# Diagonal sums moved from TensorE to GpSimd and VectorE, k tiles of the first six units loaded four tokens to a partition, and a new order of work

## The chip, the cores and the metric

The kernel runs on one core of one Trainium2 chip. The metric is the time of one execution on the device in microseconds (us), the median of several runs. A core has five engines that run their own instruction queues: TensorE (PE, with its weight loads listed apart as PEld), VectorE (DVE), ScalarE (ACT), GpSimd (POOL) and SyncE (SP). They share the on-chip memory SBUF; matmul results land in PSUM, eight banks of 128 x 512 f32. DMA transfers between HBM and SBUF are issued from the queues of SP, POOL and ACT.

## The reference

Two stages. The first is a linear-attention recurrence with a decay per channel (4 batches, 8 heads, 768 tokens, head size 48); the second is a feed-forward block with a squared ReLU (384 to 2048 to 384).

```python
for t in range(S):
    cur = np.einsum('bhd,bhe->bhde', u[None] * kt, vt)
    y[:, :, t] = np.einsum('bhd,bhde->bhe', rt, state + cur)
    state = w[None, :, :, None] * state + np.einsum('bhd,bhe->bhde', kt, vt)
...
h = x @ w_in
g = np.maximum(h, 0.0) ** 2
out = g @ w_out
```

`x` is `y` with the heads side by side: 3072 tokens by 384.

## The kernel before

**Tiling.** The tokens are cut into chunks of 128. There are 6 chunks times 4 batches = 24 units, numbered `i`, chunk by chunk, the four batches of a chunk next to each other. A unit holds 128 tokens on the partitions and 8 heads x 48 = 384 columns.

**A unit's attention steps.** `load` brings r, k and (units 0 to 5) v by SP; from unit 6 on `load_v` brings v by POOL, after a one-column copy named `gate` that waits until the k tile of the unit before has landed. `scale` (DVE, L470/L473) multiplies r and k by powers of w and writes them in bf16 into `rkw`. `rkw` is turned so that channels lie on the partitions: units 0 to 5 by TensorE (`turn`, L499) with two ACT copies out of PSUM (`evict_rk`), later ones by a DMA transpose (`turn_dma`, L488). The result is `rkT`. `at` (L521, 8 matmuls) forms the products of all token pairs, and `mask` (DVE, L533, twice) keeps those with the key earlier than the query.

The diagonal term, a token's own key and value, is made apart from that. `rk` (DVE, L513) multiplies the r half of `rkT` by the k half, and four matmuls in `sums` (L541) contract that with `uwb`, which holds u times w. This gives one sum per token and head in the same PSUM bank as the chunk's state sums (L546). `diag_v` (DVE, L555) multiplies v by it. `state_add`, `state_decay` (DVE, L559, L563) and `state_cast` (ACT, L567) carry the state on. `y_mm` (L576, L582) forms y, `evict_y` (DVE, L591) adds the diagonal term and gives `yb`, and `yb` is turned into `xT` by TensorE (units 0 to 5, L607 and L611) or by DMA (L600).

**The feed-forward steps.** `mm1` (L623) runs in 96 groups, each a PSUM bank of 512 columns; then `relu` on ACT (L631) and `square` on ACT (L638) or, for one in four, on DVE (L640). `mm2` (L647; L663 for the last unit) has four groups of four matmuls for each unit, then an ACT copy (L654) and a store from SP.

**Weights.** Eight weight transfers (`weights`, L454 to L460) are issued from POOL. Each comes after a one-column `gate` copy that waits for one of the first loads, listed in `FRONT`.

**What sets the order.** A planner at build time (`Plan`) lists every step with its engine, a cost and what it needs. It plays the list through and writes each engine's instructions in the order so found. An engine executes its queue strictly in that order. A step's due time is its `rank`, replaced for some steps by a number in the table `TURNS`. Until a set planned time, TensorE's queue is filled with matmuls on a constant tile (`fill`, L404) wherever nothing is ready; each such matmul stays in the queue as an instruction. `room` limits how many buffers of each kind are alive.

Of the kernel before, what the change touches and what calls it, by code (L numbers as in the profile page):

```python
# [166 lines left out]
def kernel(  # L167
# [11 lines left out]
    nc = tc.nc  # L179
# [9 lines left out]
    NPE = 6  # L189
    NPY = 6  # L190
# [5 lines left out]
        "I": {  # L196
            0: 144.24, 1: 1, 2: 2, 3: 4
        },
        "rt": {
            0: -131.984, 1: -82.502, 10: 20.43, 11: 21.618, 12: 25.547, 13: 27.498, 17: 47.129, 18: 50.413, 2:  # L200
            -71.138, 20: 58.225, 21: 61.113, 22: 65.692, 23: 68.66, 3: -70.253, 4: -15.411, 5: -7.144, 6: -9.444, 7:
            -6.312
        },
        "kt": {
            0: -136.858, 1: -115.745, 11: 20.876, 16: 39.093, 17: 48.35, 19: 50.948, 2: -73.584, 21: 62.596, 3:
            -25.052, 4: -13.87, 5: -1.455, 7: 11.897
        },
        "vt": {
            0: -88.087, 1: -127.327, 2: -116.777, 3: -14.463, 4: -11.435
        },  # L210
        "sadd": {
            0: -35.242, 12: 43.151, 17: 67.289, 18: 102.058, 6: 13.355, 9: 51.499
        },
        "at": {
            10: 28.41, 15: 48.663, 2: -1012.58, 21: 75.098, 22: 80.521, 23: 97.568, 3: -57.886, 5: -85.117, 9: 73.42
        },
        "dv": {
            11: 56.999, 12: 34.611, 18: 78.368, 2: -30.837, 3: -9.083, 7: -23.381, 9: 47.89
        },
        "scale": {  # L220
            (11, 0): 45.098, (18, 0): 85.344, (23, 0): 137.198, (3, 1): 16.099, (7, 1): 36.154
        },
        "sums": {
            11: 42.348, 15: 32.285, 18: 118.116, 20: 60.674, 21: 90.506, 22: 104.529, 3: -90.968, 4: -96.114, 7:
            36.606
        },
        "stb": {
            11: 51.142, 12: 48.384, 15: 79.952, 18: 64.365, 19: 104.678, 3: -21.476, 8: 67.092
        },
        "xturn": {  # L230
            3: -95.414
        },
        "xT": {
            3: -7.841, 7: 22.027
        },
        "turn": {
            (4, 1): -1019.11, (5, 1): -65.755
        },
        "rkT": {
            (4, 0): 27.124  # L240
        },
        "sdec": {
            11: 61.243, 14: 47.641, 5: 39.993, 7: 39.494, 9: 46.764
        },
        "mask": {
            (16, 0): 82.669, (8, 0): 37.716
        },
        "y": {
            11: 43.284, 12: 43.282, 13: 71.578, 19: 65.5, 22: 88.724, 9: 26.437
        },  # L250
        "rk": {
            11: 57
        },
        "yb": {
            12: 49.359, 17: 87.282
        },
        "vb": {
            14: 76.055, 16: 78.861, 22: 86.101
        },
        "relu": {  # L260
            (0, 1): 29.661, (1, 2): 26.789, (10, 7): 52.135, (12, 5): 79.181, (16, 7): 91.168, (18, 3): 87.004, (2,
            1): 27.188, (2, 2): -7.03, (20, 0): 75.975, (20, 2): 81.329, (6, 0): 46.77, (7, 1): 40.936, (8, 1):
            30.757, (8, 6): 69.828
        },
# [10 lines left out]
        },  # L275
# [8 lines left out]
        },  # L284
        "out": {
            0: 23, 1: 27.877, 10: 69.852, 11: 74.396, 12: 68.581, 13: 44.909, 15: 66.178, 2: 31.669, 7: 43.746, 9:
            60.995
        },
        "sq": {
            (1, 2): 73.636, (10, 6): 70.251, (14, 3): 47.259, (16, 3): 88.397, (16, 5): 101.673, (18, 4): 49.326,  # L290
            (20, 0): 71.116, (20, 1): 86.752, (20, 2): 83.213, (6, 2): 58.323, (7, 1): 11.056, (8, 2): 53.53
        },
        "osb": {
            11: 86.148, 16: 91.532, 8: 76.964
        },
        "O": {
            0: 3, 1: 5, 2: 6, 3: 7
# [3 lines left out]
        ("I", 1, ("kt", 3)), ("I", 2, ("rt", 1)), ("O", 0, ("rt", 4)), ("I", 3, ("vt", 0)),  # L301
        ("O", 1, ("rt", 4)), ("O", 2, ("kt", 4)), ("O", 3, ("vt", 4)), ("I", 0, ("vt", 2)),
# [69 lines left out]
    wfour = const.tile([128, 4, 2, D], F32)  # L372
# [3 lines left out]
    spread = {}  # L376

# [21 lines left out]
    gate = const.tile([128, 1], F32)  # L399

# [52 lines left out]
    def weights(gated, q, which):  # L453
        nc.gpsimd.tensor_copy(gate, tiles[gated[1]][gated[0]][:, 0, :1])  # L454
# [7 lines left out]
    def pair(x):  # L462
        return x.rearrange("p (a o) d -> p a o d", o=2)

    def scale(i, x):
        t = tiles[i]
        t["rkw"] = rkw_b[i % NPAD]
        if x or i >= NPE:
            src, wx = (t["kt"], wneg) if x else (t["rt"], wpos)
            nc.vector.tensor_tensor(t["rkw"][:, x, :, :, :D], pair(src), pair(wx), ALU.mult)  # L470
        else:
            got = t["rt"].rearrange("p (o l) d -> p l o d", o=2)
            nc.vector.tensor_tensor(t["rkw"][:, 0, :, :, :D], got, wfour, ALU.mult)  # L473

    def load_v(i):
        c, b = units[i]
        nc.gpsimd.tensor_copy(gate, tiles[i - 1]["kt"][:, 0, :1])  # L477
# [23 lines left out]
    def evict_rk(i, x):  # L501
        t = tiles[i]
        if x:
            nc.scalar.copy(t["rkT"][:, 1], t["tp", 1])  # L504
        else:
            nc.scalar.copy(
                t["rkT"][:, 0].rearrange("p a (q l) -> p a q l", l=4), t["tp", 0].rearrange("p l (q a) -> p a q l", a=HP)
            )

# [25 lines left out]
    def sums(i):  # L535
# [3 lines left out]
        t["d"] = bank("s", i)[:, dm : dm + H]  # L539
        for p in range(HP):  # L540
# [4 lines left out]
        for p in range(HP if c < NCH - 1 else 0):  # L545
# [3 lines left out]
                start=False, stop=(p == HP - 1), skip_group_check=True,  # L549
# [148 lines left out]
    add("w", ACT, 1.08, power_four, rank=-1e3, needs=["w0"])  # L698
    add("wk", ACT, 0.48, do(power, wneg, down), rank=-999, needs=["log", "w"], uses=[("log", n) for n in range(4)])
# [7 lines left out]
    for n, (what, q, gated) in enumerate(FRONT):  # L707
# [3 lines left out]
        )  # L711
    for i in range(NU):
# [4 lines left out]
        for n, name in enumerate(("rt", "kt", "vt") if i < NPE else ("rt", "kt")):  # L717
            swift = n == 0 and i < NPE
# [5 lines left out]
        for x in range(2):  # L724
            add(
                ("scale", i, x), DVE, 0.47, do(scale, i, x), rank=a - 4 + 0.1 * x,
                needs=[("rt", i) if x == 0 else ("kt", i), "wk" if x else ("w" if i < NPE else "wr"), ("scale", i - 1, x) if i else None],
# [149 lines left out]
```

## Time and profile before

| | |
|---|---|
| median of 3 runs | 178.01 us (176.65 to 178.38) |
| the profiled execution's own time | 177.58 us |
| its span, first to last instruction | 175.8 us |
| granted TensorE clock | 1.00 throughout |
| DMA traffic | 28.88 MB, 86838 packets, of which 77632 are under 512 bytes |

The page of the profile sums each engine's busy time and lists groups of equal instructions with their count, busy time and mean duration. A view by windows gives each engine's busy time in chosen stretches; a timeline lists instructions in order of time. A matmul's listed duration holds a latency that the next matmul overlaps: four matmuls of one kind in a row are listed with 0.39 us and eight with 0.62 us, so that each further one takes about 0.06 us. The same holds for DVE, whose listed 0.55 us for a 384-column instruction is 0.47 us from one start to the next. Costs are therefore taken from one start to the next.

### The profile page before, as it was taken

Reading aid. Unit: us, or ns where it says so; the run is one execution under the profiler, and the core shown is the slowest. Engines: PE = TensorE matmul, PEld = TensorE weight load, DVE = VectorE, ACT = ScalarE, POOL = GpSimd, SP = SyncE. Lnnn points to the kernel's source line nnn. Section 1 sums busy time; section 2 is a strip of 40 time slices with the busy share of each in tenths; the row PEclk is TensorE's granted clock in tenths of the full one; section 3 lists DMA queues with packets and bytes.
Section 4 is the critical chain, followed back from the end, with each engine's and each line's share of the span. In section 5 each row is a group of like instructions: output and inputs, shape, how many; then the busy total and the mean of one; then the engine's idle time right before and its main releaser. Section 6 shows DMA issues by size and latency. Waiting matters only on the chain.

```text
span 175.8 us, 5172 instructions
## 1 busy us (share of the span) xinstructions
PE 168.0 (96%) x2096; PEld 131.8 (75%) x2096; DVE 120.9 (69%) x244; ACT 129.8 (74%) x264; POOL 34.8 (20%) x80
## 2 busy tenths in 40 slices
PE   6997999899999999999999999999999999999992
PEld 5986888777777777787876776866866977777972
DVE  3277977745699999987979878889896356540300
ACT  3628799997749396799797595795894897584950
POOL 7570090005402220203213023202211000000000
PEclk9999999999999999999999999999999999999999
DMA  4989999999999999899899999995999924031022
GB/s 111 204 160 191 230 152 212 184 205 188 134 183 165 193 173 206 181 164 215 188 206 177 270 202 194 150 240 130 209 185 151 313 54 132 4 110 24 4 92 87
DMA packets 86838, 28.88 MB, mean 164 GB/s; under 512 B 77632, under 2 KB 85952, under 8 KB 86816
## 3 DMA queue, kind: packets, MB, share of 16 engines
q1 hardware_dynamic: 81744, 21.83, 67.5%
q0 software_dynamic: 4928, 6.69, 21.4%
q8 instruction: 16, 0.26, 0.6%
q14 instruction: 6, 0.05, 0.1%
q10 hardware_dynamic: 144, 0.05, 0.1%
HBM read 20.50 MB, written 4.72 MB: 143 GB/s over the span
## 4 chain that ended last, share of the span: by engine, by line
PE 62%; DMA 24%; SPq 5%; DVE 3%; POOL 2%; issue 2%; ACT 1%; DVEq 0%; POOLq 0%
PE bank L623 28%; PE bank L647 25%; DMA w_out_q<-in_moe_w_out_dram 8%; DMA kt<-in_k_dram 6%; DMA xT<-yb 5%; DMA rkT<-rkw 4%; SPq L448 3%; PE bank L521 2%; SPq L450 2%; PE bank L576 2%; PE bank L663 2%; PE bank L582 1%; POOL w_out_q L460 1%; PE bank L546 1%; PE bank L541 1%
## 5 line engine op out<-in xcount | busy, mean ns | idle before, releaser
L623 PE MATMUL bank<-xT,w_in_q 128*128 128x128 bf16 (+1 forms) x864 | 71.7, 237 | 1.0 <-ACT xT L611 0.5
L631 ACT ACTIVATE gr<-bank 128x512 f32<-128x512 f32 x96 | 54.6, 609 | 21.9 <-PE bank L623 21.9
L647 PE MATMUL bank<-w_out_q,g 128*128 128x384 bf16 x368 | 68.0, 326 | 0.3 <-DMA w_out_q<-in_moe_w_out_dram 0.3
L623 PEld LDWEIGHTS <-w_in_q 128*128 128x128 bf16 x864 | 61.0, 98 | 7.0 <-issue 0.8
L647 PEld LDWEIGHTS <-g 128*128 128x128 bf16 x368 | 33.5, 98 | 19.1 <-issue 0.4
L638 ACT ACTIVATE g<-gr 128x512 bf16<-128x512 f32 x72 | 45.1, 650 | 0.7
L533 DVE TENSOR_TENSOR am<-bank,smask 128x512 bf16<-128x512 f32 x48 | 31.4, 683 | 8.6 <-PE bank L521 8.1
L640 DVE TENSOR_TENSOR g<-gr 128x512 bf16<-128x512 f32 x24 | 16.5, 686 | 14.6 <-ACT gr L631 14.5
L477 POOL COPY gate<-kt 128x1 f32<-128x1 f32 x18 | 5.2, 290 | 81.1 <-DMA kt<-in_k_dram 81.1
L470 DVE TENSOR_TENSOR rkw<-kt,wneg 128x384 bf16<-128x384 f32 x24 | 13.2, 551 | 6.6 <-ACT wneg L416 3.4
L479 POOL DMA_DIRECT2D vt<-in_v_dram x18 | 15.9, 884 | 4.2 <-issue 1.3
L567 ACT CAST stb<-st 128x384 bf16<-128x384 f32 x20 | 10.6, 528 | 7.9 <-DVE st L559 4.4
L654 ACT COPY osb<-bank 128x384 f32<-128x384 f32 x23 | 11.1, 483 | 5.4 <-PE bank L647 5.3
L555 DVE TENSOR_TENSOR dv<-vb,bank 128x384 f32<-128x384 bf16 x24 | 13.0, 547 | 2.8 <-PE bank L546 1.6
L513 DVE TENSOR_TENSOR rk<-rkT 128x512 bf16<-128x512 bf16 x24 | 10.1, 419 | 6.9 <-ACT rkT L504 4.9
L591 DVE TENSOR_TENSOR yb<-bank,dv 128x384 bf16<-128x384 f32 x24 | 13.2, 550 | 1.9 <-PE bank L582 1.4
L483 ACT CAST vb<-vt 128x384 bf16<-128x384 f32 x24 | 12.5, 520 | 0.0
L404 PE MATMUL bank<-warm 128*128 128x128 bf16 x116 | 11.0, 268 | 1.1 <-DVE warm L342 1.1
L470 DVE TENSOR_TENSOR rkw<-rt,wpos 128x384 bf16<-128x384 f32 x18 | 9.9, 550 | 1.0 <-DMA rt<-in_r_dram 1.0
L404 PEld LDWEIGHTS <-warm 128*128 128x128 bf16 x116 | 9.6, 124 | 1.3 <-DVE warm L342 1.1
L521 PE MATMUL bank<-rkT 64*128 64x128 bf16 x192 | 9.6, 220 | 0.2 <-DMA rkT<-rkw 0.2
L521 PEld LDWEIGHTS <-rkT 64*128 64x128 bf16 x192 | 5.5, 95 | 5.6 <-issue 3.7
(71 smaller groups left out, 123.1 us busy)
## 6 DMA issues: line engine op xcount, KB each, us to landing
kt<-in_k_dram SPq DMA_DIRECT2D x24, 192.0 KB, 4.2
out_dram<-osb SPq DMA_DIRECT2D x23, 192.0 KB, 2.6
rt<-in_r_dram SPq DMA_DIRECT2D x18, 192.0 KB, 4.3
vt<-in_v_dram POOLq DMA_DIRECT2D x18, 192.0 KB, 4.8
w_in_q<-in_moe_w_in_dram POOLq DMA_DIRECT2D x4, 384.0 KB, 7.4
w_out_q<-in_moe_w_out_dram POOLq DMA_DIRECT2D x4, 384.0 KB, 11.3
rt<-in_r_dram SPq DMA_DIRECT2D x12, 96.0 KB, 3.9
vt<-in_v_dram SPq DMA_DIRECT2D x6, 192.0 KB, 4.9
```

The costliest lines, as they stand in the source:

```text
L404: nc.tensor.matmul(out=banks[0][:, :128], lhsT=warm, rhs=warm, start=True, stop=True)
L470: nc.vector.tensor_tensor(t["rkw"][:, x, :, :, :D], pair(src), pair(wx), ALU.mult)
L479: nc.gpsimd.dma_start(out=tiles[i]["vt"], in_=v[b, :, c * C : (c + 1) * C, :].rearrange("h s d -> s h d"))
L521: nc.tensor.matmul(out=t["at"][o][:, p, :], lhsT=t["rkT"][sl, 1, p, :], rhs=t["rkT"][sl, 0, p, :], start=True, stop=True,)
L533: nc.vector.tensor_tensor(am, t["at"][o], smask.unsqueeze(1).to_broadcast([C, HP, C]), ALU.mult)
L555: nc.vector.tensor_tensor(t["dv"], t["vb"], t["d"].unsqueeze(2).to_broadcast([C, H, D]), ALU.mult)
L591: nc.vector.tensor_tensor(t["yb"], t["y"], t["dv"].rearrange("p h d -> p (h d)"), ALU.add)
L623: nc.tensor.matmul(out=t["h", s][:, a], lhsT=turned, rhs=chunks[c]["xT"][:, n, b : b + m, :], start=(n == 0), stop=(n == NK - 1),)
L631: nc.scalar.activation(t["gr", s], t["h", s], AF.Relu)
L638: nc.scalar.activation(g, x, AF.Square)
L640: nc.vector.tensor_tensor(g, x, x, ALU.mult)
L647: nc.tensor.matmul(out=t["o"], lhsT=chunks[units[i][0]]["g"][:, f, units[i][1], :], rhs=w_out_q[f // 4][:, f % 4, :], start=(f == 0), stop ...
```

## The change

Three things are done, and all queues are put in a new order.

1. The k tiles of units 0 to 5 are loaded as the r tiles already were: four consecutive tokens on a partition, in two transfers with 768 contiguous bytes a descriptor instead of one with 192. `scale` then multiplies k by a second set of powers with that layout (`wfour[:, 1]`), `evict_rk` restores the order of the tokens while it copies, and because the state sums need k with tokens in order, `rkT`'s k half is turned back by four matmuls (`turn_back`) and copied by ACT into `rkw` (`evict_back`). The powers are made by two DVE multiplications or additions and two ACT exponentials of 384 columns in place of four of 96.
2. From unit 6 on `rk` and the four matmuls with `uwb` are gone. GpSimd multiplies r by k and the product by u (`product`, two instructions of 128 x 384 f32), and DVE sums 48 columns at a time (`product_sum`). `diag_v` now reads that sum from SBUF, not PSUM. u is loaded once to all partitions (`load_u`, one gate and one transfer on POOL). In the last chunk, units 20 to 23, `sums` is left out altogether.
3. `TURNS` and `FRONT` are new. The gate copies read the last head's column, not the first's.

```diff
+    NKE = 6
+    ND = 6
     TURNS = {
...
     FRONT = (
-        ("I", 1, ("kt", 3)), ("I", 2, ("rt", 1)), ("O", 0, ("rt", 4)), ("I", 3, ("vt", 0)),
-        ("O", 1, ("rt", 4)), ("O", 2, ("kt", 4)), ("O", 3, ("vt", 4)), ("I", 0, ("vt", 2)),
+        ("I", 0, ("kt", 0)), ("I", 1, ("rt", 1)), ("O", 0, ("rt", 2)), ("I", 2, ("kt", 4)),
+        ("O", 1, ("vt", 4)), ("I", 3, ("kt", 3)), ("O", 2, ("vt", 3)), ("O", 3, ("rt", 5)),
     )
...
-    def power_four():
-        for l in range(4):
-            nc.scalar.activation(wfour[:, l].rearrange("p o d -> p (o d)"), lnw, AF.Exp, scale=at4[:, l : l + 1])
+    def log_at(x):
...
+    def power_four(x):
+        nc.scalar.activation(wfour[:, x].rearrange("p l o d -> p (l o d)"), lnat[x].rearrange("p l e -> p (l e)"), AF.Exp, scale=(1.0, -1.0)[x])
...
-        if name == "rt" and i < NPE:
+        if (name == "rt" and i < NPE) or (name == "kt" and i < NKE):
             src = src.rearrange("(a o) (q l) d -> o q a (l d)", o=2, l=4)
             for o in range(2):
                 nc.sync.dma_start(out=x[:, o * 4 : o * 4 + 4, :].rearrange("p l d -> p (l d)"), in_=src[o])
...
+    def load_u():
+        nc.gpsimd.tensor_copy(gate, tiles[2]["kt"][:, H - 1, :1])
+        nc.gpsimd.dma_start(out=ub, in_=u.rearrange("h d -> (h d)").unsqueeze(0).to_broadcast([128, dm]))
+
+    def product(i, x):
+        t = tiles[i]
+        flat = "p h d -> p (h d)"
+        if x == 0:
+            t["p"] = work.tile([128, dm], F32, name="p", bufs=3)
+            nc.gpsimd.tensor_tensor(t["p"], t["rt"].rearrange(flat), t["kt"].rearrange(flat), ALU.mult)
+        else:
+            nc.gpsimd.tensor_tensor(t["p"], t["p"], ub, ALU.mult)
+
+    def product_sum(i):
+        t = tiles[i]
+        t["d"] = work.tile([128, H], F32, name="d")
+        nc.vector.tensor_reduce(t["d"], t["p"].rearrange("p (h d) -> p h d", h=H), axis=mybir.AxisListType.X, op=ALU.add)
...
+    def turn_back(i):
+        t = tiles[i]
+        t["tb"] = bank("h", i, "kb").bitcast(BF16)[:, : HP * C].rearrange("p (a c) -> p a c", a=HP)
+        for p in range(HP):
+            nc.tensor.transpose(t["tb"][:, p, :], t["rkT"][:, 1, p, :], identb)
+
+    def evict_back(i):
+        t = tiles[i]
+        nc.scalar.copy(
+            t["rkw"][:, 1, :, :, :D], t["tb"].rearrange("p a (o e) -> p a o e", o=2)[:, :, :, :D]
+        )
...
-        t["d"] = bank("s", i)[:, dm : dm + H]
-        for p in range(HP):
+        if i < ND:
+            t["d"] = bank("s", i)[:, dm : dm + H]
+        for p in range(HP if i < ND else 0):
             nc.tensor.matmul(
                 out=t["d"], lhsT=t["rk"][:, p, :], rhs=uwb[:, p, :],
...
-        add(("rk", i), DVE, 0.335, do(rk, i), rank=a + 1, needs=[("rkT", i)], new=[("rk", i)], uses=[("rkT", i)])
+        if i < ND:
+            add(("rk", i), DVE, 0.335, do(rk, i), rank=a + 1, needs=[("rkT", i)], new=[("rk", i)], uses=[("rkT", i)])
+        else:
+            add(("p", i, 0), POOL, 0.85, do(product, i, 0), rank=a - 4, needs=[("rt", i), ("kt", i)], new=[("p", i)], uses=[("rt", i), ("kt", i)])
+            add(("p", i, 1), POOL, 0.85, do(product, i, 1), rank=a - 3.9, needs=[("p", i, 0), "ub"], uses=[("p", i)])
+            add(("d", i), DVE, 0.45, do(product_sum, i), rank=a, needs=[("p", i, 1)], new=[("d", i)], uses=[("p", i)])
...
-        rt=7, kt=7, vt=7, rkw=NPAD, g=2, rkT=6, vb=NVB, rk=4, am=8, dv=4, yb=4, xT=3, gr=6, osb=6,
+        rt=7, kt=7, vt=7, rkw=NPAD, g=2, rkT=6, vb=NVB, rk=4, p=3, d=4, am=8, dv=4, yb=4, xT=3, gr=6, osb=6,
```

In the built queues of the changed kernel TensorE has 107 fill matmuls where it had 116, 24 matmuls with `uwb` where it had 96, and 24 transposes of `turn_back`; DVE has 6 instructions `rk` where it had 24, and 18 sums; GpSimd has 36 products. In the old order the last fill stands just before the first `mm1` group; in the new one 19 fills stand behind that group.

More of the change, by code (lines that the diff above doesn't have):

```diff
@@ new lines @@
+            -18.789, 5: 1.255
+        },
+        "at": {
+            0: -23.571, 14: 79.514, 3: -26.806, 4: -31.171, 6: 51.213
+        },
+        "dv": {
+            1: -11.548, 13: 49.916, 5: -3.178
+        },
+        "kb": {
+            (2, 0): -33.889, 4: -8.382
+        },
+        "sums": {
+            11: 69.884, 13: 73.704, 15: 74.62, 2: -28.968, 4: 16.668, 5: -11.289, 8: -1.517
+        },
+        "stb": {
+            2: 89.988, 4: -18.771, 8: 6.116
+        },
+        "rkT": {
+            (3, 0): 53.688, 16: 48.745, 3: -6.991
+        },
@@ L210 @@
+        "xturn": {
+            3: -9.37
+        },
+        "sdec": {
+            13: 87.372, 4: -3.574
+        },
+        "y": {
+            11: 29.297, 14: 41.464, 4: 16.667, 8: 0.138
+        },
+        "xT": {
+            12: 28.896, 4: 12.144
+        },
+        "turn": {
+            (5, 0): 23.573
+        },
+        "p": {
+            (13, 0): -9.823, (14, 0): 124.821, (15, 1): 118.984, (6, 0): 135.527
         },
         "sadd": {
-            0: -35.242, 12: 43.151, 17: 67.289, 18: 102.058, 6: 13.355, 9: 51.499
+            14: 46.679, 6: 37.463
@@ L222 @@
         },
[L223 to L252, printed above, removed]
+        "d": {
+            11: -4.297
         },
         "yb": {
[L255 to L258, printed above, removed]
+            12: 70.26
@@ L371 @@
     nc.scalar.activation(lnw, wrow, AF.Ln)
-    wfour = const.tile([128, 4, 2, D], F32)
+    wfour = const.tile([128, 2, 4, 2, D], F32)
     wpos = const.tile([128, H, D], F32)
@@ L399 @@
     gate = const.tile([128, 1], F32)
+    ub = const.tile([128, dm], F32)
     def fill():
@@ L453, in weights @@
     def weights(gated, q, which):
-        nc.gpsimd.tensor_copy(gate, tiles[gated[1]][gated[0]][:, 0, :1])
+        nc.gpsimd.tensor_copy(gate, tiles[gated[1]][gated[0]][:, H - 1, :1])
         if which == "I":
@@ L548, in sums @@
                 rhs=t["vb"][:, 2 * p : 2 * p + 2, :].rearrange("p h d -> p (h d)"),
-                start=False, stop=(p == HP - 1), skip_group_check=True,
+                start=(i >= ND and p == 0), stop=(p == HP - 1), skip_group_check=True,
             )
@@ L697 @@
     add("log", PE, 0.28, spread_log, rank=-1e3, needs=["w0"], new=[("log", n) for n in range(4)])
-    add("w", ACT, 1.08, power_four, rank=-1e3, needs=["w0"])
-    add("wk", ACT, 0.48, do(power, wneg, down), rank=-999, needs=["log", "w"], uses=[("log", n) for n in range(4)])
+    for x in range(2):
+        add(("lnat", x), DVE, 0.47, do(log_at, x), rank=-1e3 + x, needs=["w0", ("lnat", 0) if x else None])
+        add(("w", x), ACT, 0.42, do(power_four, x), rank=-1e3 + x, needs=[("lnat", x)])
+    add("wk", ACT, 0.48, do(power, wneg, down), rank=-999, needs=["log", ("w", 1)], uses=[("log", n) for n in range(4)])
     add("wr", ACT, 0.48, do(power, wpos, up), rank=-998, needs=["wk"], uses=[("log", n) for n in range(4)])
@@ L711 @@
         )
+    copy("ub", POOL, 1.2, load_u, rank=10, needs=[("kt", 2)], move=(0.6, 65, 1.4, 0.0, 0.0), uses=[("kt", 2)])
     for i in range(NU):
@@ L745 @@
                 add(
-                    ("rkT", i) if x else ("rkT", i, 0), ACT, 0.46, do(evict_rk, i, x), rank=a + 0.1 * x - 0.1,
+                    ("rkT", i) if x else ("rkT", i, 0), ACT, 0.5, do(evict_rk, i, x), rank=a + 0.1 * x - 0.1,
                     needs=[("turn", i, x), ("rkT", i, 0) if x else None], uses=[("h", i, "rk", x), ("rkT", i)],
                 )
+            if i < NKE:
+                add(("kb", i, 0), PE, 0.223, do(turn_back, i), rank=a + 1, needs=[("rkT", i)], new=[("h", i, "kb")], uses=[("rkT", i)])
+                add(("kb", i), ACT, 0.4, do(evict_back, i), rank=a + 1, needs=[("kb", i, 0)], uses=[("h", i, "kb"), ("rkw", i)])
         else:
             copy(("rkT", i), SP, 1.24, do(turn_dma, i), rank=a - 30, needs=both, move=(1.5, 18, 0.67, 1.0, LATE[1]), new=[("rkT", i)], uses=[("rkw", i)])
-        add(("rk", i), DVE, 0.335, do(rk, i), rank=a + 1, needs=[("rkT", i)], new=[("rk", i)], uses=[("rkT", i)])
+        if i < ND:
+            add(("rk", i), DVE, 0.335, do(rk, i), rank=a + 1, needs=[("rkT", i)], new=[("rk", i)], uses=[("rkT", i)])
+        else:
+            add(("p", i, 0), POOL, 0.85, do(product, i, 0), rank=a - 4, needs=[("rt", i), ("kt", i)], new=[("p", i)], uses=[("rt", i), ("kt", i)])
+            add(("p", i, 1), POOL, 0.85, do(product, i, 1), rank=a - 3.9, needs=[("p", i, 0), "ub"], uses=[("p", i)])
+            add(("d", i), DVE, 0.45, do(product_sum, i), rank=a, needs=[("p", i, 1)], new=[("d", i)], uses=[("p", i)])
         if i in PAIRED:
@@ L765 @@
             )
-        add(
-            ("sums", i), PE, 0.275 if c < NCH - 1 else 0.105, do(sums, i), rank=a + (2.1 if c else 2.1),
-            needs=[("rk", i), "uwb", ("at", i)] + ([("scale", i, 1), ("vb", i)] if c < NCH - 1 else []),
-            new=[("s", i)], uses=[("rk", i), ("rkw", i)] + ([vb] if c < NCH - 1 else []),
+        if i < ND:
+            add(
+                ("sums", i), PE, 0.275, do(sums, i), rank=a + 2.1,
+                needs=[("rk", i), "uwb", ("at", i), ("kb", i) if i < NKE else ("scale", i, 1), ("vb", i)],
+                new=[("s", i)], uses=[("rk", i), ("rkw", i), vb],
+            )
+        elif c < NCH - 1:
+            add(
+                ("sums", i), PE, 0.17, do(sums, i), rank=a + 2.1, needs=[("at", i), ("scale", i, 1), ("vb", i)],
+                new=[("s", i)], uses=[("rkw", i), vb],
+            )
+        add(
+            ("dv", i), DVE, 0.465, do(diag_v, i), rank=a + 2, needs=[("sums", i) if i < ND else ("d", i), ("vb", i)],
+            new=[("dv", i)], uses=[("s", i) if i < ND else ("d", i), vb],
         )
-        add(("dv", i), DVE, 0.465, do(diag_v, i), rank=a + 2, needs=[("sums", i), ("vb", i)], new=[("dv", i)], uses=[("s", i), vb])
         if c < NCH - 1:
```

80 lines of the change are left out of this document (40 added, 40 removed), and 24 rows, old and new, of the table TURNS.

## The prediction

> **What bounds the kernel now.** First the page's busy times, then the windows, to see which engine is full where.
>
> ```profile
> span 175.8 us, 5172 instructions
> PE 168.0 (96%) x2096; PEld 131.8 (75%) x2096; DVE 120.9 (69%) x244; ACT 129.8 (74%) x264; POOL 34.8 (20%) x80
> ```
> ```profile
> core 0: us, PE busy (x) PEld busy (x) DVE busy (x) ACT busy (x) POOL busy (x), PEclk, DMA share, GB/s
> 24.00:32.00 8.00, 7.45 (x136) 6.66 (x134) 6.15 (x12) 8.00 (x19) 2.40 (x5) 1.00 1.19 192
> 48.00:56.00 8.00, 8.00 (x108) 5.96 (x105) 7.84 (x17) 5.37 (x11) 0.77 (x2) 1.00 1.18 168
> 64.00:72.00 8.00, 8.00 (x127) 6.21 (x125) 7.85 (x17) 6.28 (x14) 1.56 (x3) 1.00 1.12 185
> ```
>
> PE is the bound overall. Adding its instructions at the typical time from one start to the next (mm1 0.056 us, or 0.109 when 256 columns wide; mm2 0.163; and so on from the timeline) gives 149.6 us of needed work; fills take 11.1, stalls 10.7 (5.6 of them before 40 us), the first instruction starts at 1.1, and 3.4 lie behind the last matmul's start. That is 175.8 (after rounding). Two other engines are full for a time: ACT at 24 to 32 us, DVE at 48 to 72 us. So a gain on PE counts only where neither of these holds it back.
>
> Next, how DVE's queue runs, what four `uwb` matmuls cost, and what a GpSimd copy does beside DVE.
>
> ```profile
> 46.97 0.24 PE L541 MATMUL bank<-uwb,rk 128*128 128x8 bf16 x4
> 47.08 0.33 PE L546 MATMUL bank<-vb,rkw 128*128 128x96 bf16 x4
> ...
> 67.77 0.54 DVE L555 TENSOR_TENSOR dv<-vb,bank 128x384 f32<-128x384 bf16 x1
> 68.24 0.55 DVE L559 TENSOR_TENSOR st<-bank,st 128x384 f32<-128x384 f32 x1
> 68.70 0.54 DVE L591 TENSOR_TENSOR yb<-bank,dv 128x384 bf16<-128x384 f32 x1
> 69.17 0.41 DVE L513 TENSOR_TENSOR rk<-rkT 128x512 bf16<-128x512 bf16 x1
> 69.50 0.55 DVE L563 TENSOR_TENSOR st<-st,wend 128x384 f32<-128x384 f32 x1
> ...
> 79.41 0.56 DVE L470 TENSOR_TENSOR rkw<-kt,wneg 128x384 bf16<-128x384 f32 x1
> 79.50 0.50 POOL L477 COPY gate<-kt 128x1 f32<-128x1 f32 x1 [7.26 <-DMA kt<-in_k_dram]
> ...
> 94.15 1.29 DVE L533 TENSOR_TENSOR am<-bank,smask 128x512 bf16<-128x512 f32 x2 [0.37 <-PE bank L521]
> 94.93 0.18 POOL L477 COPY gate<-kt 128x1 f32<-128x1 f32 x1 [2.06 <-DMA kt<-in_k_dram]
> ```
>
> Four `uwb` matmuls take 0.11 us (46.97 to 47.08). DVE runs without gaps: 384 columns 0.47 us, `rk` 0.33. The one-column GpSimd copy takes 0.18 us beside `mask`, which reads one operand from PSUM, but 0.50 beside `scale`, which reads both from SBUF, and ends 0.03 us after it. So the two seem to exclude each other when DVE reads SBUF twice.
>
> **The change, part by part.**
>
> PE: 18 x 4 `uwb` matmuls go, 18 x 0.105 = 1.9 us. Six `turn_back` groups come; four more transposes take 0.22 us (listed: 0.39 for four, 0.62 for eight), 1.3 in all. Net -0.6. Fills: nine fewer, 0.06 (17 in 1.12 us) to 0.11 each (23 in 2.63), -0.7.
>
> The k loads: a packet of the hardware queue costs 175.8 x 16 x 67.5% / 81744 = 23 ns of one DMA engine, four of 192 bytes 93 ns. One of 768 bytes, by the byte price of the software queue (175.8 x 16 x 21.4% over 6.69 MB = 0.09 ns), costs 69. 256 packets a tile on 16 engines: 0.4 us a tile, 2.3 over six tiles; nothing if bytes alone decide, 6.6 if packets alone do. The gain lies in the first 20 us, before ACT is full. `load_u` gives back about 1 us (192 KB, like a k tile) and one gate and issue on POOL.
>
> ACT: six `evict_back` copies at about 0.4 us (nearest: ACT's 384-column copies, 0.48 listed, 0.37 from start to start; bounds 0.36 to 0.48) add 2.4 us; two wide exponentials for four narrow ones change nothing. Four of the six stand behind the first `relu`, so 1.6 us fall into the stretch in which ACT is full. That eats most of the earlier start. I put the front's stalls at -0.3, bounds -2.5 (the whole k gain) and +1.6 (only the copies). The two DVE steps on the powers lie in DVE's idle time before 6 us.
>
> DVE: 18 sums over 384 columns replace 18 `rk`. The trace has no such reduction; a 384-column instruction takes 0.47 (nearest by columns), and as it reads one operand it may come down to the 0.33 of `rk`. I take 0.46: +0.13 each, 2.3 us in all, nothing where DVE has idle time. DVE is not idle between the y steps of units 5 and 11. By the queues and these durations it had 27.0 us of work for 27.1 of PE there, and in the new order has 29.2 for 31.0. So 1.8 us of cover is left.
>
> GpSimd: 36 products of two f32 operands, 128 x 384. Rows: memset of 384 columns 0.42; copy of 192 columns 0.34; a 4-column product 0.20. The copy's slope (0.14 over 192) doubled for two operands gives 0.20 + 0.56 = 0.76; bounds 0.48 (one operand) to 1.1 (0.3 more for a wait like that of the gate). Per unit with gate (0.2) and issue (0.9) GpSimd has 2.6 of some 6 us: not a bound. The Trainium skill (GPSIMD Engine Reference, Performance versus the Vector engine) gives 4.5 us for a 2048-column product and advises VectorE for plain arithmetic; by it one would take about 1.0, an estimate, and the loss below would be a third larger; no trace here shows it.
>
> Now what these products do to DVE. Of a unit's 5.1 us on DVE, 2.5 read SBUF twice (two `scale` 0.94, `state_decay` 0.47, one square 0.60, and `diag_v` 0.47, which now takes its sum from SBUF). If a product runs, a DVE instruction of this kind must wait for its end. Half the time DVE holds the port as the product comes due: the product then waits, starts as that instruction ends, and half of the next ones lose 0.76. Otherwise a rest of about 0.25 us passes and half of the next lose 0.5. That is 0.25 x 0.76 + 0.25 x 0.5, some 0.3, with repeats 0.35 us a product, 0.7 a unit; bounds 0 (DVE always wins) and 0.76 a product. Between units 5 and 11 twelve products cost 4.2 against 1.8 of cover and some 0.4 by which `mask` is ahead of y: +2.0. Units 11 to 17 have 5.6 us to spare: nothing. Units 17 to 20 have 0.6 (15.6 of work, 16.2 of PE): six products, 2.1, of which I count 1.0, as DVE comes there with some lead. Together +3.0.
>
> New waits: behind `product_sum`, waiting for POOL, stand `scale`, masks and yb on DVE. Behind a product, waiting for r and k, stands the next v load. Behind an SP load that waits until a product has read the buffer stand transposes and stores; with seven buffers of each, nothing unless GpSimd is two units late.
>
> Sum against 175.8: -0.6 - 0.7 - 0.3 + 3.0 = +1.4, a span of 177.2. The profiled execution took 177.58 and the median is 178.01; I add 1.5 to the median: 179.5.
>
> **The rivals.**
>
> *Only GpSimd loses* (faster). The rows show GpSimd waiting for DVE, never DVE for GpSimd. Then 3.0 drops out: 176.4. Against it: things that exclude each other should block in both orders. The Trainium skill (SBUF — State Buffer, Who interferes with whom) says that a VectorE instruction with two SBUF inputs and a GpSimd instruction that reads SBUF hold the port in turn, and the second to issue waits for the whole of the first; the gate's 0.50 us agrees for one order, and no run here shows the other.
>
> *The front wins* (faster). ACT's extra copies fit into its waits (it idles most of the first 16 us), the full 2.3 us of DMA count and little of the port's loss comes through: 178 - 1.3 - 2.3 + 0.5 = 174.9. Against it: ACT 8.00 of 8 at 24 us.
>
> *The port costs more* (slower). At 1.0 us a product and 0.5 lost on each, 12 products cost 6.0 less 2.2, six cost 3.0 less 0.6: +6.2, less 1.6 from the front and PE: 182.6. It decides once a product takes over 0.9, or late sums hold up DVE's queue.
>
> **How the numbers follow.** Chances: forecast 0.36, only GpSimd loses 0.20, the front wins 0.16, the port costs more 0.28. Within 1% (176.2 to 179.8; about what runs of this kernel, 176.65 to 178.38, can tell) lie 0.22 of the forecast and 0.12 of the first rival. Faster: 0.16, 0.08 of the first rival and 0.02 of the forecast, 0.26. Slower: 0.28 and 0.12, 0.40. The likeliest time is 179.5, its own range 177.5 to 181.5. The range 175 to 183.2 leaves out about a tenth at each end.
>
> **What would show it.** `scale`, `state_decay`, squares and the new `diag_v` listed well over their 0.55 and 0.68 us where a product runs, while masks and yb stay; products of 0.7 to 1.1 us; more PE stalls at y from 50 to 85 us; PE's first `mm1` before 18.47 us, and ACT full from then on. I am wrong if DVE's listed durations do not move, or if ACT still has gaps between 20 and 40 us.

## The result and the profile after

The changed kernel takes 196.4 us, median of four runs (194.94 to 196.54), beside 178.19 for the kernel before on the same chip. The ratio is 1.103, with a 95% interval of 1.095 to 1.111: slower by a tenth, where 179.5 was forecast and 183.2 was the end of the range. (Ratios, here and below, leave disturbed runs out, so that a median can lie above its ratio, and the ratio of the write-only run below rests on two of its ten runs.) The profiled execution took 194.94 us, with a span of 193.0 and a mean granted clock of 0.98.

The page's busy times first.

```profile
span 193.0 us, 5119 instructions
...
PE 170.0 (88%) x2039; PEld 130.2 (67%) x2039; DVE 148.0 (77%) x246; ACT 131.2 (68%) x268; POOL 77.4 (40%) x118
```

The two numbers to compare with the page of before are DVE's: 246 instructions after 244, and 148.0 us after 120.9. The removed `rk` (18 x 0.42 listed) and the added sums (18 x 0.54) explain 2.1 us of these 27. The groups by line and shape, with the count behind the x, then busy time and mean ns, show where the rest sits. `scale` is now L472, `mask` L564, `square` on DVE L672, `diag_v` L587, `evict_y` L623, `state_decay` L595, `product_sum` L492.

```profile
L564 DVE TENSOR_TENSOR am<-bank,smask 128x512 bf16<-128x512 f32 x48 | 31.1, 680 | 2.0 <-PE bank L552 1.8
L672 DVE TENSOR_TENSOR g<-gr 128x512 bf16<-128x512 f32 x24 | 20.1, 843 | 16.7 <-ACT gr L663 16.7
L472 DVE TENSOR_TENSOR rkw<-rt,wpos 128x384 bf16<-128x384 f32 x18 | 17.3, 963 | 0.6 <-DMA rt<-in_r_dram 0.6
L472 DVE TENSOR_TENSOR rkw<-kt,wneg 128x384 bf16<-128x384 f32 x18 | 15.4, 856 | 2.3 <-DMA kt<-in_k_dram 2.3
L587 DVE TENSOR_TENSOR dv<-vb,d 128x384 f32<-128x384 bf16 x18 | 14.7, 816 | 1.6 <-ACT vb L502 1.6
L623 DVE TENSOR_TENSOR yb<-bank,dv 128x384 bf16<-128x384 f32 x24 | 13.1, 548 | 1.9 <-PE bank L614 1.9
L595 DVE TENSOR_TENSOR st<-st,wend 128x384 f32<-128x384 f32 x16 | 12.0, 753 | 0.2
L492 DVE TENSOR_REDUCE d<-p 128x8 f32<-128x384 f32 x18 | 9.7, 539 | 0.0
```

These were 551 ns for `scale` of k, 550 for `scale` of r, 547 for `diag_v`, 550 for `state_decay` and 686 for `square` before. Every group listed here that reads two operands from SBUF has grown, by 0.16 to 0.41 us an instruction. The masks (680 after 683) and `evict_y` (548 after 550), which read one operand from PSUM, have not moved, and the sum, which reads one, takes what a 384-column instruction takes.

The same view for GpSimd has the two products of each unit from 6 on; the third number after the bar is its idle time.

```profile
L487 POOL TENSOR_TENSOR p<-p,ub 128x384 f32<-128x384 f32 x18 | 20.2, 1122 | 0.7
L485 POOL TENSOR_TENSOR p<-rt,kt 128x384 f32<-128x384 f32 x18 | 19.8, 1102 | 40.3 <-DMA kt<-in_k_dram 31.2 <-DMA rt<-in_r_dram 6.5 <-DVE g L672 2.5
```

Next the windows, with the columns that the prediction shows.

```profile
core 0: us, PE busy (x) PEld busy (x) DVE busy (x) ACT busy (x) POOL busy (x), PEclk, DMA share, GB/s
8.00:16.00 8.00, 4.32 (x63) 3.98 (x61) 3.69 (x9) 2.82 (x6) 3.07 (x8) 0.79 0.96 196
24.00:32.00 8.00, 7.93 (x135) 6.76 (x133) 6.50 (x14) 8.00 (x18) 2.71 (x6) 1.00 1.24 209
48.00:56.00 8.00, 7.43 (x100) 5.56 (x97) 8.00 (x12) 4.99 (x10) 5.53 (x6) 1.00 0.59 97
56.00:64.00 8.00, 5.13 (x32) 2.75 (x31) 5.63 (x11) 2.19 (x5) 2.62 (x4) 0.79 1.02 125
...
104.00:112.00 8.00, 6.31 (x59) 4.46 (x57) 8.00 (x8) 1.83 (x4) 7.67 (x8) 1.00 0.91 151
```

At 48 to 56 us DVE is full with 12 instructions where it had 17. At 104 to 112 it is full with eight, GpSimd is nearly full too, PE goes short and ACT almost idle: those two engines hold each other up and everyone else waits for them. At 8 to 16 and 56 to 64 us, where PE has gaps, its granted clock is 0.79; it was 1.00 throughout before.

PE's time, added up from starts as in the prediction: needed work 149.1 us (149.6 before), fills 9.0 (10.2), stalls 30.4 (11.6), the rest unchanged. Time beyond 0.2 us behind a fill is counted as a stall here; the prediction's 11.1 and 10.7 put it with the fills, which in the new trace would hide a wait of 3.7 us for a `scale`, from 9 to 13 us. The difference is 18.8 - 1.2 - 0.4 = 17.2 us, which is what the span has grown by. The front is not to blame: at 48 us PE had done 31.1 us of needed work, 1.0 more than before. All of the loss comes after that, where the products run.

Now one such loss, in the timeline (start, duration, engine).

```profile
144.60 0.18 POOL L496 COPY gate<-kt 128x1 f32<-128x1 f32 x1
144.72 0.93 POOL L498 DMA_DIRECT2D vt<-in_v_dram  x1
144.91 2.18 DVE L472 TENSOR_TENSOR rkw<-rt,wpos 128x384 bf16<-128x384 f32 x1
...
145.66 1.01 POOL L487 TENSOR_TENSOR p<-p,ub 128x384 f32<-128x384 f32 x1
...
147.01 0.54 DVE L472 TENSOR_TENSOR rkw<-kt,wneg 128x384 bf16<-128x384 f32 x1
```

`scale` starts 0.75 us *before* the product, while GpSimd still issues the v load, and yet ends only 0.42 after the product's end: it took 2.18 us in place of 0.55. So it waited for the rest of an issue and for a whole product behind it. Sorting the DVE instructions by what ran on GpSimd as they began, nine that began within an issue with a product queued behind it lost 12.7 us (1.41 each, duration less the shortest of the kind), 19 that began within a product lost 13.1 (0.69 each), one other 0.8. That is 26.6 us over 36 products, 0.74 a product.

### The profile page after: what moved, and what is told of

Read it like the earlier page. It is cut to its first block, busy times and chain, and to the rows that moved or that the text cites. A ratio compares the mean times of both kernels' runs of the same rounds, so it can differ in the third digit from the quotient of the medians.

```text
span 193.0 us, 5119 instructions
## 1 busy us (share of the span) xinstructions
PE 170.0 (88%) x2039; PEld 130.2 (67%) x2039; DVE 148.0 (77%) x246; ACT 131.2 (68%) x268; POOL 77.4 (40%) x118
## 5 line engine op out<-in xcount | busy, mean ns | idle before, releaser
L679 PE MATMUL bank<-w_out_q,g 128*128 128x384 bf16 x368 | 69.6, 331 | 4.2 <-DVE g L672 2.6
L485 POOL TENSOR_TENSOR p<-rt,kt 128x384 f32<-128x384 f32 x18 | 19.8, 1102 | 40.3 <-DMA kt<-in_k_dram 31.2
L672 DVE TENSOR_TENSOR g<-gr 128x512 bf16<-128x512 f32 x24 | 20.1, 843 | 16.7 <-ACT gr L663 16.7
L564 DVE TENSOR_TENSOR am<-bank,smask 128x512 bf16<-128x512 f32 x48 | 31.1, 680 | 2.0 <-PE bank L552 1.8
L487 POOL TENSOR_TENSOR p<-p,ub 128x384 f32<-128x384 f32 x18 | 20.2, 1122 | 0.7
L472 DVE TENSOR_TENSOR rkw<-rt,wpos 128x384 bf16<-128x384 f32 x18 | 17.3, 963 | 0.6 <-DMA rt<-in_r_dram 0.6
L472 DVE TENSOR_TENSOR rkw<-kt,wneg 128x384 bf16<-128x384 f32 x18 | 15.4, 856 | 2.3 <-DMA kt<-in_k_dram 2.3
L496 POOL COPY gate<-kt 128x1 f32<-128x1 f32 x18 | 6.4, 357 | 25.5 <-DMA kt<-in_k_dram 25.5
L587 DVE TENSOR_TENSOR dv<-vb,d 128x384 f32<-128x384 bf16 x18 | 14.7, 816 | 1.6 <-ACT vb L502 1.6
L623 DVE TENSOR_TENSOR yb<-bank,dv 128x384 bf16<-128x384 f32 x24 | 13.1, 548 | 1.9 <-PE bank L614 1.9
L608 PE MATMUL bank<-vb,am 128*128 128x48 bf16 x192 | 10.1, 185 | 4.8 <-DVE am L564 4.7
L502 ACT CAST vb<-vt 128x384 bf16<-128x384 f32 x24 | 12.8, 532 | 1.2 <-DMA vt<-in_v_dram 1.2
L608 PEld LDWEIGHTS <-am 128*128 128x128 bf16 x192 | 8.1, 98 | 7.4 <-DVE am L564 6.7
```

Source lines behind the costliest of these rows:

```text
L485: nc.gpsimd.tensor_tensor(t["p"], t["rt"].rearrange(flat), t["kt"].rearrange(flat), ALU.mult)
L487: nc.gpsimd.tensor_tensor(t["p"], t["p"], ub, ALU.mult)
L564: nc.vector.tensor_tensor(am, t["at"][o], smask.unsqueeze(1).to_broadcast([C, HP, C]), ALU.mult)
L587: nc.vector.tensor_tensor(t["dv"], t["vb"], t["d"].unsqueeze(2).to_broadcast([C, H, D]), ALU.mult)
L608: nc.tensor.matmul(out=y[:, 2 * p + o, :], lhsT=t[f"am{o}"][:, p, :], rhs=t["vb"][:, 2 * p + o, :], start=(o == 0 and p == 0), stop=c == 0 ...
L672: nc.vector.tensor_tensor(g, x, x, ALU.mult)
```

## The experiments

Three theories were tested. **A**: a GpSimd product reading SBUF and a DVE instruction reading two SBUF operands exclude each other, whichever is first, and DVE's waits are the loss. **B**: the sums come late, because GpSimd is slow and has a longer queue. **C**: the new order, or the k loads, is at fault.

**Idle products in the kernel before.** Eighteen pairs of products are added behind the v issues, on tiles that are there from the start; nothing reads them. No other queue differs, so B and C can have no part in it.

```diff
 # the kernel before, in load_v, behind the dma_start
+        flat = "p h d -> p (h d)"
+        p = work.tile([128, dm], F32, name="p", bufs=3)
+        nc.gpsimd.tensor_tensor(p, wpos.rearrange(flat), wneg.rearrange(flat), ALU.mult)
+        nc.gpsimd.tensor_tensor(p, p, wpos.rearrange(flat), ALU.mult)
```

> The kernel before with 36 GpSimd products of 128 x 384 f32 (both operands constants in SBUF, results never read), two behind each v load; every other queue is unchanged and the diagonal sums stay on TensorE. Theory A (a GpSimd product and a VectorE instruction with two SBUF operands exclude each other, in both orders): VectorE's busy time rises by 20 to 28 us, and the time by 8 to 16 us, to 186 to 194, though nobody needs the products. Theory B (the loss is the wait for late sums in VectorE's queue): no sums, so 178 to 180 and VectorE's durations as before. Theory C (the new order or the k part): 178.

Measured: 195.8 us, 1.098 (1.090 to 1.105). The kernel before, with 36 products that nobody uses, is as slow as the changed kernel. Its busy times and three of its DVE groups:

```profile
PE 173.3 (89%) x2096; PEld 133.6 (68%) x2096; DVE 146.1 (75%) x244; ACT 130.7 (67%) x264; POOL 77.4 (40%) x116
```
```profile
L470 DVE TENSOR_TENSOR rkw<-kt,wneg 128x384 bf16<-128x384 f32 x24 | 24.1, 1003 | 4.6 <-ACT wneg L416 3.2 <-DMA kt<-in_k_dram 1.3
L644 DVE TENSOR_TENSOR g<-gr 128x512 bf16<-128x512 f32 x24 | 23.4, 977 | 13.3 <-ACT gr L635 13.3
...
L595 DVE TENSOR_TENSOR yb<-bank,dv 128x384 bf16<-128x384 f32 x24 | 13.1, 548 | 0.9 <-PE bank L586 0.8
```

DVE is busy 25.2 us longer with the very same 244 instructions; `scale` of k takes 1003 ns in place of 551, `evict_y` what it took. PE's stalls are 31.8 us.

**Idle memsets in their place.** To see whether it is a busy GpSimd or its reading that counts, six memsets of the same buffer, which only write, replace each pair.

```diff
-        nc.gpsimd.tensor_tensor(p, wpos.rearrange(flat), wneg.rearrange(flat), ALU.mult)
-        nc.gpsimd.tensor_tensor(p, p, wpos.rearrange(flat), ALU.mult)
+        for n in range(6):
+            nc.gpsimd.memset(p, 1.0)
```

> The same, but in place of each pair of products six GpSimd memsets of 128 x 384 f32, about as much GpSimd time, which read nothing from SBUF. Theory A: VectorE's durations as before, 178 to 180. Theory B, in the form that GpSimd's time delays the v loads behind it: slow like the run with the products.

Measured: 179.47 us, 1.008 (1.005 to 1.012). Its busy times and the same groups:

```profile
PE 167.1 (94%) x2096; PEld 130.5 (74%) x2096; DVE 120.5 (68%) x244; ACT 129.9 (73%) x264; POOL 81.0 (46%) x188
```
```profile
L643 DVE TENSOR_TENSOR g<-gr 128x512 bf16<-128x512 f32 x24 | 16.5, 688 | 14.3 <-ACT gr L634 14.1
L470 DVE TENSOR_TENSOR rkw<-kt,wneg 128x384 bf16<-128x384 f32 x24 | 13.3, 553 | 5.4 <-ACT wneg L416 3.2 <-DMA kt<-in_k_dram 2.0
```

GpSimd is busier than with the products (81.0 against 77.4), and DVE is untouched. GpSimd's time as such costs 0.8%; its reading of SBUF costs the other nine per cent.

**Memsets in the changed kernel.** The same swap in the changed kernel: each product becomes three memsets, so that the products of r, k and u are left out, while GpSimd stays as busy and the sums still have to wait for it. B expected it to stay slow.

```diff
-            nc.gpsimd.tensor_tensor(t["p"], t["rt"].rearrange(flat), t["kt"].rearrange(flat), ALU.mult)
-        else:
-            nc.gpsimd.tensor_tensor(t["p"], t["p"], ub, ALU.mult)
+        for n in range(3):
+            nc.gpsimd.memset(t["p"], 1.0)
```

> The changed kernel with all queues in the same order, but each product replaced by three GpSimd memsets of the same tile (about 1.1 us), so that the diagonal sums are taken over a constant; the products of r, k and u are left out. Theory A: the lost time comes back, 176 to 180, VectorE's busy time falls from 148 to about 122 us. Theory B: GpSimd's time and VectorE's wait for the sums remain, 190 to 196. Theory C: 190 to 196.

Measured: 1.004 (0.999 to 1.009) of the time before, with 123.5 us on DVE. All ten runs lie between 178.58 and 190.09 us; even their median, 183.62, is 12.8 us under the changed kernel's. The loss is gone though GpSimd is as busy (82.5 us), and though DVE now does wait for the memsets before its sums (waiting instruction, whom for: us in total, times, longest):

```profile
DVE d L491 <- POOL p L486: 7.3, 7, 2.0
```

In the changed kernel DVE never waits there: the line of `product_sum` above has 0.0 us of idle time before it. B falls: a late sum is not what costs.

**k loads and order without the products.** The k loads stay and the diagonal goes back to TensorE for all units; the planner then works with the new tables on other steps.

```diff
-    ND = 6
+    ND = 24
```

> The changed kernel with the diagonal sums of all units on TensorE as before: only the k layout of units 0 to 5 and the new order are left (the planner fits the order to the changed steps). Theory A: near the kernel before, 175 to 180, VectorE's busy time about 121 us. Theory C: most of the loss stays, over 190.

Measured: 190.21 us, 1.068 (1.060 to 1.076). DVE is as before (120.1 us busy), and PE's stalls are 25.0. Taken alone this looks like support for C, as if two thirds of the loss (0.068 of 0.103) came without any product. Two further runs were needed to read it.

The first keeps the changed kernel's own queues, but leaves the products out, so that the sums add up a tile of u.

```diff
-        t = tiles[i]
-        flat = "p h d -> p (h d)"
-        if x == 0:
...
+        tiles[i]["p"] = ub
```

> The changed kernel with all queues in its order, without the 36 products: the sums are taken over the tile that holds u, so the products of r, k and u are left out and VectorE waits for nobody there. It prices the rest of the change, forecast at -1.6 us: 175 to 178 with VectorE's busy time at 122 to 124. If the rest of the change costs time too: 179 or more.

Measured: 178.15 us, 0.995 (0.990 to 1.000). In the order made for them, all other parts of the change together cost nothing; they win some 0.9 us, with an interval that reaches to none. The second takes out the k loads as well. `TURNS` and `FRONT` are left of the change, and a few small steps: the load of u, the new way of making the powers and the gates' column.

```diff
-    NKE = 6
-    ND = 6
+    NKE = 0
+    ND = 24
```

> The new tables of due times with the steps of the kernel before: neither k part nor products. The run with the k part alone took 190. If the tables, fitted to other steps, made that loss, this one is slow as well, 183 to 192. If the k layout made it, 177 to 180; but the changed kernel without products, which has the k layout, took no longer than the kernel before.

Measured: 188.83 us, 1.064 (1.056 to 1.071), PE stalls 21.5. The small steps are also in the run without products, which lost nothing. So the tables of due times alone, laid over the old steps, cost as much as in the run with the k loads. That run measured tables that did not fit its steps, and not the k loads; C falls as a cause of the 18 us. What the k loads are worth by themselves, in an order fitted to them, was not measured.

**One product a unit.** Half of the idle products are taken out of the first experiment.

```diff
         nc.gpsimd.tensor_tensor(p, wpos.rearrange(flat), wneg.rearrange(flat), ALU.mult)
-        nc.gpsimd.tensor_tensor(p, p, wpos.rearrange(flat), ALU.mult)
```

> The kernel before with one idle product instead of two behind each v load (18 in all). If each product costs VectorE its own wait, VectorE's busy time rises by about half of the 25 us, to 132 to 136; the time rises by less than half of the 18 us, as part of the wait is covered: 181 to 187. If a few unlucky products did it all, it stays over 190.

Measured: 1.030 (1.019 to 1.041), median 184.66, DVE 133.6 us. Half the products make half of DVE's waits (12.7 of 25.2 us) but a third of the loss in time.

**A gap behind the issue.** The timeline above suggests that a product takes hold of the port, the access to SBUF that DVE and GpSimd exclude each other from, when GpSimd's sequencer hands it on, while it still stands behind the running issue. A tiny memset that the product has to wait for, since both write the same buffer, should keep it from being handed on until the issue is over. It adds work and removes none.

```diff
         p = work.tile([128, dm], F32, name="p", bufs=3)
+        nc.gpsimd.memset(p[:, :8], 1.0)
         nc.gpsimd.tensor_tensor(p, wpos.rearrange(flat), wneg.rearrange(flat), ALU.mult)
```

> The kernel before with the same 36 idle products, but an 8-column memset of the product's tile stands between the v load's issue and the first product, which must wait for it. In the run without this gap, VectorE instructions with two SBUF operands that began during the issue waited for the rest of the issue and the product behind it (1.7 to 2.2 us). If the port is taken as soon as the product is handed on, behind the running issue, then with the gap such instructions keep their 0.55 us when they begin early in the issue, VectorE's busy time falls from 146 by 4 to 7 us and the time by 2 to 5 us. If the issue itself holds the port, nothing changes: 195 to 197.

Measured: 184.81 us, 1.043 (1.032 to 1.053): by the ratios 0.055 of 178, some 10 us, faster than without the memset, with DVE at 134.0 us, 12.1 fewer. Both are well more than was expected. The same place in the timelines of the two kernels, first without the memset:

```profile
54.30 0.93 POOL L479 DMA_DIRECT2D vt<-in_v_dram  x1
54.58 2.10 DVE L567 TENSOR_TENSOR st<-st,wend 128x384 f32<-128x384 f32 x1
...
55.24 1.01 POOL L482 TENSOR_TENSOR p<-wpos,wneg 128x384 f32<-128x384 f32 x1
```

and with it:

```profile
49.25 0.92 POOL L479 DMA_DIRECT2D vt<-in_v_dram  x1
...
49.29 0.55 DVE L470 TENSOR_TENSOR rkw<-kt,wneg 128x384 bf16<-128x384 f32 x1
...
49.76 0.55 DVE L596 TENSOR_TENSOR yb<-bank,dv 128x384 bf16<-128x384 f32 x1
...
50.16 0.12 POOL L482 MEMSET p<- 128x8 f32 x1
50.22 0.55 DVE L470 TENSOR_TENSOR rkw<-kt,wneg 128x384 bf16<-128x384 f32 x1
50.37 1.25 POOL L483 TENSOR_TENSOR p<-wpos,wneg 128x384 f32<-128x384 f32 x1
```

Without it `state_decay`, begun within the issue, takes 2.10 us. With it `scale`, begun within an issue, takes its 0.55, and the second `scale` holds the product up instead (1.25 us). Over the trace, 12 DVE instructions that began within an issue had lost 15.6 us; now none does, and 25 that began within a product lose 15.6 in all.

**The gap in the changed kernel.** There the products do not always stand behind an issue. Both were first put in the place of the first, as one step,

```diff
-        else:
             nc.gpsimd.tensor_tensor(t["p"], t["p"], ub, ALU.mult)
```

> The changed kernel, all other queues in its order, with both products of a unit issued together at the place of the first. A control for the next run: only GpSimd's queue changes. The waits stay, about 28 us on VectorE: 192 to 198.

and then the memset was added to that.

```diff
             t["p"] = work.tile([128, dm], F32, name="p", bufs=3)
+            nc.gpsimd.memset(t["p"][:, :8], 1.0)
```

> The same with an 8-column GpSimd memset of the product's tile in front of each pair, which the first product must wait for. If taking the port behind a running issue makes nearly half of VectorE's waits (12.7 of 28 us began during an issue in the changed kernel), as the run before with idle products and such a gap says, VectorE's busy time falls from 148 to 132 to 138 us and the time to 183 to 188. If in the real chain the late sums count instead, it stays over 192.

Measured: 190.63 us, 1.073 (1.064 to 1.083) for the pairs, and 187.01, 1.043 (1.034 to 1.053) with the memset. The pairs alone came out below what was expected: fewer products now start right behind an issue (8 in place of 16), and waits begun within an issue fell from 12.7 to 7.2 us. With the memset there are none, DVE falls from 143.9 to 135.4 us, and the ratio by 0.030. That is the best found with the products on GpSimd, and it is still 4% slower than before.

**The products on DVE itself.** Same places, same operands, other engine.

```diff
-            nc.gpsimd.tensor_tensor(t["p"], t["rt"].rearrange(flat), t["kt"].rearrange(flat), ALU.mult)
+            nc.vector.tensor_tensor(t["p"], t["rt"].rearrange(flat), t["kt"].rearrange(flat), ALU.mult)
...
-            nc.gpsimd.tensor_tensor(t["p"], t["p"], ub, ALU.mult)
+            nc.vector.tensor_tensor(t["p"], t["p"], ub, ALU.mult)
```

> The changed kernel, same order, with the 36 products on VectorE at the same places instead of on GpSimd. VectorE gets 36 x 0.47 = 17 us more work, but no waits: busy time about 140, against 148 with the waits. Theory A: faster than the changed kernel, 183 to 192; slower than the kernel before, because VectorE is full from 48 to 80 us. If the products' place in the order were at fault, it is no faster than 195.

Measured: 179.39 to 185.02 us in four runs, too wide a spread for a ratio. Its busy times in the execution that took 179.39:

```profile
PE 167.7 (94%) x2039; PEld 130.3 (73%) x2039; DVE 138.2 (78%) x282; ACT 131.3 (74%) x268; POOL 39.6 (22%) x82
```

The same kernel was run again.

> The changed kernel with the products on VectorE once more, since its four times lay between 179.4 and 185.0. Theory A: 179 to 184, faster than the changed kernel by 12 us or more though VectorE does 17 us more work, and not faster than the kernel before.

Measured: 183.23 us, 1.019 (1.010 to 1.028). DVE does 36 more instructions and is still 9.8 us less busy than in the changed kernel (138.2 against 148.0), and the kernel takes 1.019 of the time before in place of 1.103, some 15 us less. Taking the products off DVE costs DVE more than doing them.

Of the kernels that leave nothing out, none beats the kernel before. The run without any products sets what the change could have won at about half a per cent.

## Why the prediction was wrong

Wrong were the forecast, no change that can be told from noise, and the range; slower had the largest of the three chances (0.40), but its rival stood at 182.6, a loss of under 5 us and not 18. The mechanism that the forecast names, DVE and GpSimd excluding each other where both read SBUF, is the one that the first two experiments show; its price was off by a factor of two. Step by step:

**The step that failed** is the price of a product: "half the time DVE holds the port as the product comes due", and with it "0.35 us a product, 0.7 a unit; bounds 0 and 0.76". Measured are 0.74 a product, 1.5 a unit. Two things made it up. A product alone takes 1.01 us (median; shortest 0.99), where the slope of the copy gave 0.76. And DVE is shut out not from the product's start, but while it still waits behind the issue, a stretch of 0.93 us that the working left out. In the changed kernel sixteen products start right behind a v load's issue. Fifteen of them held DVE up, nine with an instruction that began within the issue (1.41 us each); together they cost 1.06 us a product, and the other twenty 0.44. The idle products show the same: 1.05 for the eighteen behind an issue, 0.48 for those that follow them, and 0.43 for all 36 with the memset. The prediction's own working gives 0.46 with 1.0 us put for 0.76. So its halves were about right, its product was a quarter too short, and the stretch behind the issue is what it missed. The memset experiment measures this part by itself: 12 of the 25 us that DVE loses to idle products, and 10 of the 17 us of time.

**The cover** was counted right between units 5 and 11 and too high behind them. Put 0.74 into the prediction's own working: twelve products between units 5 and 11 cost 8.9, less 2.2; twelve between 11 and 17 cost 8.9, less 5.6; six from 17 to 20 cost 4.4, less 0.6. That is 6.7, 3.3 and 3.8, or 13.8 us. Between the same y steps PE's stalls grew by 6.4, 8.7 and 2.9, or 18.0 us. So "units 11 to 17 have 5.6 us to spare: nothing" is the second term that failed. DVE lost 10.9 us there, and the spare time covered about 2. Counted from starts in the changed kernel's queues it comes to 3.8 us and not 5.6; why still less of it helped is open. The runs side by side show cover of this kind for the whole kernel. From DVE's added busy time (against 120.9 for the kernel before with idle products, against 123.3 in the run without products for the changed ones) to the time that the ratio gives:

| kernel | DVE's waits, us | time lost, us |
|---|---|---|
| one idle product | 12.7 | 5.4 |
| idle pairs with gap | 13.1 | 7.6 |
| changed, pairs with gap | 12.1 | 7.7 |
| changed, pairs | 20.6 | 13.0 |
| idle pairs | 25.2 | 17.4 |
| changed | 24.7 | 18.3 |

The first 13 us of waits cost about half of their length, the next 12 nearly all of it. Each time is good to between 1.3 and 2 us, and the waits fall at different places, so the table does not say where the bend lies.

**The rule and the figure that had been weighed** came out nearer than the rows. The Trainium skill (SBUF — State Buffer, Who interferes with whom) says that the second to issue waits for all of the first. The runs agree, for both orders: DVE's 2.18 us behind GpSimd, and a product of 1.25 behind `scale`. The same section exempts GpSimd instructions that only write, and the memsets agree, with 120.5 us on DVE against 120.9. The estimate of about 1.0 us a product, worked out from the Trainium skill (GPSIMD Engine Reference, Performance versus the Vector engine), fits the 1.01 measured; the page's 4.5 us is for an add of 2048 columns, and by columns alone it would give 0.84.

**The rivals.** *Only GpSimd loses* (0.20) is refuted: DVE loses 26.6 us. *The front wins* (0.16) needed the port's loss nearly to vanish; its ground that ACT idles most of the first 16 us was a misreading, since ACT was busy for 8.2 of them. *The port costs more* (0.28) had the right sign, the right product (1.0 us) and the right point, over 0.9; but it put the loss at 0.5 a product and counted nothing for the middle units, so it stopped at 182.6. Late sums, the other half of its condition, did not decide: in the changed kernel no sum was late, and the write-only run, in which some are, is not slower.

**The other terms.** PE's needed work: -0.6 forecast, -0.4 measured. Fills: -0.7 forecast, -1.2 measured, by the count of the section on the result. The sum: 0.46 us taken, 0.46 from start to start. `evict_back`: 0.4 taken, 0.36 measured. The front came out as forecast: the first `mm1` at 17.60 us in place of 18.47, ACT at 8.00 and 7.93 of 8 from 24 to 40 us, and PE 1.0 us ahead at 48, where -0.7 for the fills and -0.3 for the front's stalls had been put down. Everything but the products was forecast at -1.6 (with no contention) and measured at -0.9, with an interval from -1.7 to 0.

Of what was to show it, most came as written: the four groups grew while masks and `evict_y` stayed, and the first `mm1` came earlier. The products took 0.99 to 1.48 us where 0.7 to 1.1 was written, and the place was too narrow, since PE stalls from 48 us to 152, not to 85.

## What to carry to other kernels

Before work goes from VectorE to GpSimd, list which VectorE instructions read two operands from SBUF: a GpSimd instruction that reads SBUF may hold up one of these for all of its own time, and here a product added 0.69 us to VectorE's busy time while GpSimd made it (24.7 over 36), and 0.41 when VectorE made it itself (138.2 less 123.3, over 36). Where such a GpSimd instruction stands behind a DMA issue on its queue, put a small write that it depends on between them, or put it elsewhere. And when one part of a change is tried alone in a kernel with tables of due times that were fitted to its steps, run the tables alone too: here they cost 6% over steps that they weren't made for, and nothing over their own.

## What the runs showed of the hardware that was not expected

A GpSimd product that is queued behind a running DMA issue keeps VectorE from the shared port although it has not started. VectorE instructions with two SBUF operands that begin in that stretch end 0.4 to 0.6 us after the product's end (1.7 to 2.5 us in all; in each of the two traces one gets through ahead of the product, 0.3 or 0.5 us late), and a 0.12 us memset that the product must wait for removes the effect wholly: 12 such waits and 15.6 us in the one trace, none in the other. An issue with no product behind it does nothing of the kind: in the kernel before, `scale` begun within a v issue took 0.55 us. That the sequencer hands the product on early is the reading that fits; the traces show the waits, and not the hand-over itself.
